# One transfer per head instead of one per pair for spreading the softmax reciprocals, with PE's order searched anew

## The chip, the cores and the metric

The kernel runs on one core of one Trainium2 chip. The metric is the device time of one execution in microseconds. Before the change the median of three runs is 820.94 us (820.1 to 821.65).

## The reference

A block-causal attention (8 batches, 8 heads, 576 positions, head width 64) feeds a mixture of four single-head causal attentions, of which two are chosen per position by a gate. All data are float32.

```python
scores = scale * np.matmul(q, k.transpose(0, 1, 3, 2))
scores = np.where(pos[:, None] // 64 >= pos[None, :] // 64, scores, -1e9)
attn = exp(scores - max);  attn = attn / (sum(attn) + 1e-09)
x = (attn @ v).transpose(0, 2, 1, 3).reshape(B, S, H * D)
...
logits = x @ w_gate                      # the best 2 of 4 experts, softmax over these two
for e in range(4):
    q, k, v = x @ wq[e], x @ wk[e], x @ wv[e]
    a = causal softmax(scale * q @ k.T)
    out += gate[e] * ((a @ v) @ wo[e])
```

## The kernel before

The work comes in 48 pairs: 32 pairs of attention heads (kind "A": 8 batches of 4 pairs) and 16 pairs of experts (kind "M": 8 batches of 2). `add_attention` writes down the tasks of one pair. PE makes the scores of both heads into PSUM (`bank`), DVE masks them and takes the row minimum (`nm`), ACT takes the exponentials into `e` and sums them into `ssum`. The exponentials are transposed for the second product, either by PE (`id,e`) or, for the widest tile, by DVE within blocks (`eI`) and two transfers through DRAM (`dt<-eI`, 640 KB, then four `eTb<-dt` of 160 KB). PE then multiplies with the values into another bank, where positions lie along the free axis and the 64 columns of head 0 and of head 1 lie in partitions 0 to 63 and 64 to 127.

In that layout the division by the softmax sum needs the reciprocal of each position in every one of a head's 64 partitions. The chain for it is: ACT adds epsilon (`f_r1`, `r<-ssum`), DVE takes the reciprocal (`f_r2`) and, for experts, multiplies by the gate (`f_r3`), DVE transposes 32 x 32 blocks (`f_rt`, `rT<-r`), SP writes the result to DRAM (`f_rw`, `dr<-rT`, 16 KB), and SP reads it back spread over the partitions (`f_rd`, `rs<-dr`, 288 KB: 2304 bytes into each of 128 partitions). In DRAM head 0's 576 numbers start at 0 and head 1's at element 640. Then DVE multiplies the product in PSUM by `rs` (`f_p1`, `x<-bank,rs`), which frees the bank; `x` is rounded and its rest kept (`f_p2`, `f_p3`) for the next projections, or (`y`, `yl`) for the output projection with `woh` and `wol`.

There are three `rs` buffers and two of `r`, `rT` and `dr`; the latter come free when the transfer `rs<-dr` that reads `dr` has landed. [...]

Order: `Plan.run` is a list scheduler in Python that runs while the kernel is built. Each task has an engine, a cost, keys (`KEYS`) that set which of the ready tasks goes first, and for transfers a latency `lat` and a ring load. PE's tasks go in the order of the table `LINE`, fixed. The result is one stream per engine, executed in order: an engine that waits holds up all that stands behind it. All input transfers, the turn through `dt` and the reciprocals are issued on SP; the outputs on ACT. Where a helper issues every instruction, all have one line (L327).

## Time and profile before

| what | value |
|---|---|
| median of 3 runs | 820.94 us |
| the profiled execution | 812.63 us |
| its span, first to last instruction | 810.8 us |
| PE, DVE, ACT, POOL busy in it | 616.6, 484.3, 447.4, 185.9 us |
| mean granted TensorE clock | 0.863 |
| mean DMA rate | 150 GB/s (121.84 MB) |

The profile is of one execution. "Busy" counts instructions; a busy PE need not be at its peak, and its matmuls last longer at a lower granted clock. The table of waits says which engine stood still, and what ended its wait; the chain follows the work that ended last back to its start.

### The profile page before, as it was taken

The page shows a single profiled execution, that of the slowest core. Times are in us where ns is not written, and L with a number is a line of the kernel's source. Part 1 is how long each engine was busy: PE and PEld are TensorE (multiplying, and loading weights), DVE is VectorE, ACT ScalarE, POOL GpSimd, SP SyncE. Part 2 cuts the span into 40 slices and gives each one's busy share as a digit, 9 for nine tenths or more (in the row PEclk, how much of TensorE's full clock was granted, in tenths as well). Part 3 has the DMA queues.
Part 4 walks back from the last instruction along what each step waited for, and adds up shares of the span by engine and source line. Part 5 has one row for each costly group of instructions (what it writes and reads, how often), then busy time and mean ns, then how long its engine had stood idle before and what let it go on. Part 6 is the DMA issues. An engine that isn't in the chain of part 4 may idle for free.

```text
span 810.8 us, 19107 instructions
## 1 busy us (share of the span) xinstructions
PE 616.6 (76%) x7235; PEld 560.7 (69%) x7235; DVE 484.3 (60%) x1709; ACT 447.4 (55%) x1502; POOL 185.9 (23%) x272
## 2 busy tenths in 40 slices
PE   7668885589769689669777879696596775968964
PEld 5557784489668588569766778585595665868953
DVE  7466674478547567458665668584484554643931
ACT  6565574368537466457655656564484454543631
POOL 2243040223213123223212222031231132100101
PEclk8869997699978979789889898997798888989997
DMA  6526464546565457455654457384376434532222
GB/s 211 152 86 194 125 207 124 150 132 174 172 202 150 130 145 248 115 171 184 182 188 142 136 166 207 122 236 124 113 223 177 142 89 122 162 83 84 91 75 75
DMA packets 75884, 121.84 MB, mean 150 GB/s; under 512 B 11664, under 2 KB 56208, under 8 KB 75792
## 3 DMA queue, kind: packets, MB, share of 16 engines
q1 hardware_dynamic: 70256, 110.88, 47.1%
q10 hardware_dynamic: 5536, 9.73, 3.5%
q8 instruction: 57, 0.93, 0.5%
q14 instruction: 35, 0.29, 0.1%
HBM read 82.19 MB, written 38.40 MB: 149 GB/s over the span
## 4 chain that ended last, share of the span: by engine, by line
DMA 61%; PE 21%; DVE 9%; SPq 3%; ACT 3%; issue 2%; ACTq 0%; DVEq 0%; POOL 0%
DMA rs<-dr 35%; PE bank L327 21%; DMA dr<-rT 13%; DMA dt<-eI 8%; DMA eTb<-dt 4%; SPq L327 3%; DVE bank L327 3%; DVE x L327 2%; DMA raw<-in_qk_dram 2%; ACT e L327 1%; DVE eI L327 1%; DVE nm L327 0%; DVE r L327 0%; DVE rT L327 0%; ACT el L327 0%
## 5 line engine op out<-in xcount | busy, mean ns | idle before, releaser
L327 ACT ACTIVATE e<-bank,nm 128x448 f32<-128x448 f32 (+3 forms) x384 | 219.0, 579 | 56.8 <-DVE nm L327 54.2
L327 DVE CUSTOM_DVE_ANT_0 bank<-bank,mask_a 128x192 f32<-128x192 f32 (+3 forms) x320 | 154.3, 504 | 19.3 <-PE bank L327 13.8
L327 DVE TENSOR_TENSOR x<-bank,rs 128x256 f32<-128x256 f32 (+1 forms) x144 | 45.7, 349 | 186.4 <-DMA rs<-dr 168.0
L327 PE MATMUL bank<-hl,lo 64*128 64x320 f32 (+2 forms) x352 | 84.9, 437 | 81.8 <-DVE x L327 46.5
L327 PE MATMUL bank<-x,wh 128*128 128x320 f32 (+1 forms) x512 | 111.9, 313 | 0.1
L327 PEld LDWEIGHTS bank<-hl,lo 64*128 64x128 f32 x352 | 46.7, 219 | 88.0 <-issue 38.6
L327 PE MATMUL bank<-id,e 64*128 64x64 f32 x1381 | 71.7, 243 | 32.9 <-ACT e L327 16.2
L327 PEld LDWEIGHTS bank<-id,e 64*128 64x128 f32 x1381 | 63.9, 155 | 44.3 <-ACT e L327 19.8
L327 POOL TENSOR_TENSOR lo<-raw,hl 128x320 fp32r<-128x320 f32 x77 | 65.7, 878 | 124.1 <-ACT hl L327 71.1
L327 PEld LDWEIGHTS bank<-x,wh 128*128 128x128 f32 x512 | 87.1, 200 | 6.3 <-issue 2.5
L327 POOL TENSOR_TENSOR x<-x,x 128x256 fp32r<-128x256 f32 (+1 forms) x55 | 43.6, 798 | 199.3 <-ACT x L327 106.9
L327 PE MATMUL bank<-eTb,va 128*64 128x64 f32 (+2 forms) x1136 | 71.4, 284 | 16.9 <-DMA eTb<-dt 16.0
L327 DVE CUSTOM_DVE_ANT_0 bank<-bank,mask_c 128x448 f32<-128x448 f32 (+4 forms) x160 | 77.6, 501 | 10.7 <-PE bank L327 7.5
L327 PEld LDWEIGHTS bank<-eTb,va 128*64 128x64 f32 x1136 | 67.7, 150 | 21.3 <-ACT x L327 9.4
L327 PE MATMUL bank<-x,wl 128*128 128x320 f32 (+1 forms) x256 | 78.2, 306 | 0.0
L327 ACT ACTIVATION_READ_ACCUMULATOR e<-bank,nm 128x1 f32 x384 | 78.0, 203 | 0.0
L327 PE MATMUL bank<-lo,hl 64*128 64x320 f32 (+2 forms) x352 | 70.4, 354 | 0.0
L327 PE MATMUL bank<-hl 64*128 64x320 f32 (+2 forms) x352 | 70.2, 353 | 0.0
L327 DVE STREAM_TRANSPOSE eI<-e 128x1024 f32<-128x1024 f32 x86 | 61.6, 754 | 11.9 <-DMA dt<-eI 9.3
L327 DVE DVE_READ_ACCUMULATOR2_ANT nm<- 128x1 f32 (+1 forms) x480 | 66.9, 139 | 0.0
L327 PE MATMUL bank<-wh,x 128*128 128x260 f32 x288 | 61.9, 295 | 0.0
L327 PE MATMUL bank<-raw 64*128 64x64 f32 (+4 forms) x320 | 48.9, 398 | 15.4 <-DVE x L327 9.7
(113 smaller groups left out, 1232.6 us busy)
## 6 DMA issues: line engine op xcount, KB each, us to landing
dt<-eI SPq DMA_DIRECT2D x43, 640.0 KB
eTb<-dt SPq DMA_DIRECT2D x172, 160.0 KB
va<-in_v_dram SPq DMA_DIRECT2D x32, 576.0 KB
raw<-in_qk_dram SPq DMA_DIRECT2D x31, 576.0 KB
rs<-dr SPq DMA_DIRECT2D x48, 288.0 KB
out_dram<-ob ACTq DMA_DIRECT2D x32, 256.0 KB
raw<-in_w_dram SPq DMA_DIRECT2D x4, 386.0 KB
out_dram<-ob ACTq DMA_DIRECT2D x8, 128.0 KB
```

Source lines behind the costliest of these rows:

```text
L327: r = f(*args, **kwargs)
```

## The change

`f_rd` issues two transfers, one for each head: 64 partitions from head 0's numbers, then 64 partitions from head 1's. Before, one transfer read both by a pattern whose outermost dimension has size 2. The bytes are the same. The planner's cost of the task on SP goes from 620 to 1150 ns, its latency and load stay. `KEYS` and `LINE` are replaced by tables found for these costs, so tasks move on every engine.

```diff
@@ KEYS, LINE: all numbers new @@
     0, 1, 4, 3, 2, 12, 7, 10, 5, 6, 11, 13, 18, 14, 15, 8, 19, 20, 9, 16, 28, 17, 
-    ... 21, 22, 27, 26, 23, 25, 29, 31, 30, 35, 24, 34, 32, 33, 42, 37, 43, 36,
+    ... 22, 21, 27, 26, 23, 24, 25, 29, 31, 30, 35, 34, 33, 32, 36, 43, 37, 42,
...
         def f_rd(e):
             rs, dr = rs_[rsb.idx], dr_[rb.idx]
-            nc.sync.dma_start(rs, bass.AP(tensor=dr.tensor, offset=dr.offset, ap=[[640, 2], [0, 64], [1, S]]))
+            for h in range(2):
+                nc.sync.dma_start(rs[64 * h:64 * h + 64], bass.AP(tensor=dr.tensor, offset=dr.offset + 640 * h,
+                                                                  ap=[[0, 64], [1, S]]))
...
         t_ = plan.add("S", 570, f_rw, n_, deps=(t_,), lat=1000, load=150)
-        rd = plan.add("S", 620, f_rd, n_, deps=(t_,), get=(rsb,), rel=(rb,), lat=1800, load=900)
+        rd = plan.add("S", 1150, f_rd, n_, deps=(t_,), get=(rsb,), rel=(rb,), lat=1800, load=900)
```

SP, where two pairs issue their `rs` back to back (136 to 147 us in the profile before). Before:

```order
L327 DMA dr_143<-rT_141 4x32x32
L327 DMA dr_142<-rT_140 4x32x32
L327 DMA rs_136<-dr_143 128x1x576
L327 DMA rs_137<-dr_142 128x1x576
L327 DMA va_112<-in_v_dram 128x1152
L327 DMA dt_111<-eI_108 128x4x320
L327 DMA va_113<-in_v_dram 128x1152
```

After:

```order
L327 DMA dr_143<-rT_141 4x32x32
L327 DMA dr_142<-rT_140 4x32x32
L327 DMA rs_136<-dr_143 64x576 x2
L327 DMA rs_137<-dr_142 64x576 x2
L327 DMA dt_111<-eI_108 128x4x320
L327 DMA va_113<-in_v_dram 128x1152
```

Each `rs` is issued in two pieces, and `dt_111` moves ahead of a load of values.

DVE at the same place, where it reads these two `rs` (ISA rows are the masking and the minimum). Before:

```order
L327 TENSOR_TENSOR x_133<-bank_147,rs_135 128x256
L327 ISA bank_149,nm<-bank_149,mask_c 128x448
L327 ISA nm 128x1
L327 TENSOR_TENSOR x_117<-x_133,x_117 128x256
L327 TENSOR_TENSOR x_134<-bank_146,rs_136 128x64
L327 TENSOR_TENSOR x_134<-bank_146,rs_136 128x256
L327 TENSOR_TENSOR x_133<-bank_146,rs_137 128x64
L327 TENSOR_TENSOR x_133<-bank_146,rs_137 128x256
L327 ISA bank_147,nm<-bank_147,mask_c 128x192
```

After:

```order
L327 TENSOR_TENSOR x_133<-bank_148,rs_135 128x256
L327 ISA bank_149,nm<-bank_149,mask_c 128x448
L327 ISA nm 128x1
L327 ISA bank_147,nm<-bank_147,mask_c 128x448
L327 TENSOR_TENSOR x_134<-bank_147,rs_136 128x64
L327 TENSOR_TENSOR x_134<-bank_147,rs_136 128x256
L327 TENSOR_TENSOR x_133<-bank_149,rs_137 128x64
L327 TENSOR_TENSOR x_133<-bank_149,rs_137 128x256
L327 ISA bank_146,nm<-bank_146,mask_c 128x192
```

The multiplications stay side by side, right ahead of the next masking; a subtraction (`x_117`) no longer stands between them and banks change.

PE at that place: the last product before its next scores. Before:

```order
L327 MATMUL bank_147<-eTb_107,va_113 64x128
L327 MATMUL bank_147<-eTb_107,va_113 64x256
L327 MATMUL bank_147<-eTb_107,va_113 64x128 x4
L327 MATMUL bank_147<-eTb_107,va_113 64x64 x3
L327 MATMUL bank_149<-hl_76,lo_78 128x320
L327 MATMUL bank_146<-hl_76,lo_78 128x320
```

After:

```order
L327 MATMUL bank_146<-eTb_107,va_113 64x128
L327 MATMUL bank_146<-eTb_107,va_113 64x256
L327 MATMUL bank_146<-eTb_107,va_113 64x128 x4
L327 MATMUL bank_146<-eTb_107,va_113 64x64 x3
L327 MATMUL bank_148<-hl_76,lo_78 128x320
L327 MATMUL bank_149<-hl_76,lo_78 128x320
```

Here PE's sequence stays and only the banks differ; the scores still write a bank that a multiplication by `rs_137` reads shortly before (146 before, 149 after).

## The prediction

> **What bounds the kernel now.** I read the page's head and its chain first.

> ```profile
> span 810.8 us, 19107 instructions
> PE 616.6 (76%) x7235; PEld 560.7 (69%) x7235; DVE 484.3 (60%) x1709; ACT 447.4 (55%) x1502; POOL 185.9 (23%) x272
> DMA rs<-dr 35%; PE bank L327 21%; DMA dr<-rT 13%; DMA dt<-eI 8%; DMA eTb<-dt 4%; SPq L327 3%; DVE bank L327 3%; DVE x L327 2%; DMA raw<-in_qk_dram 2%; ACT e L327 1%; DVE eI L327 1%; DVE nm L327 0%; DVE r L327 0%; DVE rT L327 0%; ACT el L327 0%
> ```

> No engine is full: PE, the fullest, idles 810.8 − 616.6 = 194 us. The transfer that the change touches is 35% of the chain (284 us), more than PE's work. The table of waits (total us, times, longest) says whom it holds up:

> ```profile
> DVE x L327 <- DMA rs<-dr: 168.0, 33, 10.3
> PE bank L327 <- DVE x L327: 87.1, 22, 9.7
> ACT r L327 <- DMA rs<-dr: 64.2, 13, 9.3
> PE bank L327 <- ACT e L327: 32.5, 13, 8.6
> PE bank L327 <- DMA eTb<-dt: 22.2, 5, 7.0
> PE bank L327 <- ACT eTb L327: 15.6, 6, 5.5
> PE bank L327 <- ACT vm L327: 8.5, 2, 6.8
> PE bank L327 <- POOL ytl L327: 6.2, 1, 6.2
> PE bank L327 <- DVE gsm L327: 4.9, 1, 4.9
> ```

> DVE stands 168 us for `rs`, mean 5.1; PE stands 87 us for the multiplication behind it. ACT stands 64 us because `r` has two buffers, which come free when an older `rs` has landed, and ACT's exponentials stand behind that. One such place in the timeline (start, duration, instruction, idle before it), and the end of the kernel:

> ```profile
> 139.90 1.11 SPq L327 DMA_DIRECT2D rs<-dr  x2
> 149.37 0.56 DVE L327 TENSOR_TENSOR x<-bank,rs 128x64 f32<-128x64 f32 x2 [5.38 <-DMA rs<-dr]
> 155.64 0.56 DVE L327 TENSOR_TENSOR x<-bank,rs 128x64 f32<-128x64 f32 x2 [5.71 <-DMA rs<-dr]
> 156.26 0.64 PE L327 MATMUL bank<-hl,lo 64*128 64x320 f32 x2 [9.68 <-DVE x L327]
> ...
> 778.80 1.18 SPq L327 DMA_DIRECT2D rs<-dr  x2
> 789.51 0.42 DVE L327 TENSOR_TENSOR x<-bank,rs 128x256 f32<-128x256 f32 x1 [10.00 <-DMA rs<-dr]
> 795.50 0.89 DVE L327 TENSOR_TENSOR x<-bank,rs 128x256 f32<-128x256 f32 x3 [5.56 <-DMA rs<-dr]
> ```

> Two `rs` issued half a microsecond apart come 6.27 us apart, and 5.99 us apart at the end, where little else moves. So one `rs` takes 6.0 us of transfer by itself: 288 KB in 6.0 us is 49 GB/s. What a transfer can do here, and what a small one costs, is in the pieces of the chain (start, us from issue to landing) and in the sizes of the page:

> ```profile
> 180.02 4.51 DMA dt<-eI
> 245.19 8.20 DMA rs<-dr
> 777.50 1.96 DMA dr<-rT
> ...
> dt<-eI SPq DMA_DIRECT2D x43, 640.0 KB
> rs<-dr SPq DMA_DIRECT2D x48, 288.0 KB
> dr<-rT SPq DMA_DIRECT2D x48, 16.0 KB
> ```

> 640 KB of `dt<-eI` land 4.51 us after issue, 288 KB of `rs` never sooner than 8.20 in the listed chain, 16 KB in 1.96. `rs` is slow in itself, not for its bytes: it runs on a few of the 16 DMA engines. With 1.96 taken as the fixed part, `dt<-eI` moves 640 KB in 2.55 us, 251 GB/s; at a sixteenth of that per engine (15.7 GB/s), or somewhat more when unhindered, 49 GB/s is two or three engines. The DRAM pattern of `rs` begins with a dimension of size 2, that of `dt` with 128.

> [...]

> **The change part by part.** *Landing of `rs`.* Bounds for the new one from rows: best, 1.96 fixed + 288 KB at 251 GB/s = 1.15 + one more issue; worst, today's 8.2 and more. The issue:

> ```profile
> L327 SPq DMA_DIRECT2D rs<-dr x48: 502/520/3337, 21.3 to 779.5; - x48
> ```

> So 1.96 + 1.15 + 0.52 = 3.6 us. I take 3.6, since the new pattern is like that of `dt` with its partitions outermost. That is 4.6 us less than 8.2, and over 5 less than the usual 9 to 10.

> *DVE and PE.* 33 waits of 5.1 us in the mean, nearly all shorter than 5 to 6, mostly vanish. Of PE's 87.1 us behind them I take nine tenths: 78. Of the waits for `ACT e` (32.5), and for `eTb`, `vm`, `ytl`, `gsm` (15.6 + 8.5 + 6.2 + 4.9 = 35.2) about half stand behind a DVE or ACT that waited for `rs`: 34. Bounds here: none of it, or all 68.

> *The other transfers.* All of SP's traffic shares the 16 engines:

> ```profile
> q1 hardware_dynamic: 70256, 110.88, 47.1%
> 336.32 6.84 SPq L327 DMA_DIRECT2D va<-in_v_dram  x2
> ```

> If `rs` sits on two engines, it holds these for 48 × 6.0 = 288 us, on top of the rest of the traffic, at most 47% of 811 = 381: up to 82% busy where the mean is half. Whatever spreads over all 16 waits for its share on these two, and SP itself is held while issuing (6.84 us for two loads, against 0.35 or so). I take half of PE's 22.2 us for `eTb`: 11. Bounds 0 and 22.

> *Clock.* The table by 20 us windows (PE, PEld, DVE, ACT, POOL busy with counts, granted clock, DMA share, GB/s): the first is a window with stalls, the others are all with PE busy 18 us or more.

> ```profile
> 140.00:160.00 20.00, 10.32 (x134) 9.48 (x133) 8.01 (x29) 6.33 (x20) 4.78 (x7) 0.73 0.42 126
> 100.00:120.00 20.00, 18.41 (x252) 16.80 (x248) 15.26 (x57) 14.05 (x48) 8.11 (x12) 0.88 0.67 207
> 180.00:200.00 20.00, 20.00 (x207) 18.37 (x205) 16.97 (x60) 17.91 (x64) 6.63 (x8) 1.00 0.64 184
> 300.00:320.00 20.00, 20.00 (x292) 18.29 (x290) 17.59 (x65) 16.20 (x55) 7.03 (x11) 1.00 0.80 237
> 420.00:440.00 20.00, 18.44 (x249) 16.15 (x248) 12.71 (x48) 12.47 (x43) 5.34 (x8) 0.95 0.68 192
> 580.00:600.00 20.00, 18.92 (x209) 17.65 (x210) 17.09 (x61) 15.64 (x52) 7.87 (x12) 0.85 0.59 181
> 700.00:720.00 20.00, 18.25 (x217) 16.43 (x217) 12.29 (x45) 10.99 (x39) 0.00 (x0) 1.00 0.59 158
> 760.00:780.00 20.00, 19.11 (x207) 17.02 (x207) 17.34 (x67) 13.27 (x49) 1.71 (x3) 1.00 0.32 105
> ...
> core 0: 810.8 us, clock 0.863
> ```

> Dense windows get 0.95 in the mean, the stalled one 0.73, the whole 0.863. With two thirds of the stalls gone I take 0.92 as the new mean. [...]

> *What is given back.* 48 more issues of 0.52 us are 25 us of SP, which lie beside SP's waits except for the 0.52 counted in each landing; without that cover they are 25 us. The next limits are near: in dense windows DVE and ACT are busy 12 to 18 of 20 us, `dt` and `eTb` are 12% of the chain (97 us), `dr<-rT` still comes ahead of each `rs` with 1.96 us or more. I take a quarter of the 123 us of stalls as coming back under other names: 31. Bounds 0 and about half, 61.

> *The new order* of PE moves few kinds of work at the places shown; I count nothing for it, bounded by the spread of the give-back.

> Sum, on the profiled execution: 812.6 − 78 − 34 − 11 − 19 + 31 = 701.6. The runs' median is 8.3 us above that execution: 710 us.

> **The rivals.** *Another wait takes over.* The turn through `dt` and `eTb`, or DVE's own work, ends the waits instead, and the clock stays. Then only about half of PE's 87 us is won: 812.6 − 44 + 8 = 777. For it speaks that the 43 turns stay as long as `dr` and `dt` queue; against it, that those landings suffer from `rs` as well.

> *PE gets full.* In the seven dense windows 1633 matmuls ran in 140 us; 7235 at that rate take 620 us. With 20 us of start and end and the 8 us: 648. Against it: three engines at 85% or more in order seldom stay so.

> *The halves follow one another, slower.* If the 49 GB/s come from reading the same row of DRAM over and over and not from the number of engines, two transfers gain nothing, and each lands one issue later: 284 us of chain at about 9.7 us a piece are 29 pieces, and 29 × 0.52 = 15 us make 836; if each half in turn takes the full 6 us, 29 × 6 more make 995. It decides if two `rs` still come 6 us apart. Against it: nothing else in the trace is so slow for its bytes, but no other transfer repeats one row, so it can't be excluded. [...]

> **How the numbers follow.** Forecast (670 to 750): 0.62. Another wait (750 to 800): 0.18. PE full (635 to 670): 0.12. Halves follow one another: 0.05. The remaining 0.03 is a gain under 20 us or none, 0.01 of it within 0.2% (what a measurement can tell here) and 0.01 slower by an unlucky order. So faster 0.93, same 0.01, slower 0.06. The range 660 to 785 leaves out the lower part of "PE full", the far end of "another wait" and the slow cases, about 2 in 10; its ends are the sum with all of its terms at their better bounds cut back by half, and 777 with the noise of the runs.

> **What would show it.** Right: `rs` lands 3 to 4.5 us after its second issue, two in a row come 1 to 2 us apart, DVE's wait for `rs` falls under 50 us, PE is busy 82 to 88% of the span at a clock over 0.9, and `dt<-eI` lands in 5 us more often. Wrong on the mechanism: still 6 us between two `rs`. Wrong on the size: `rs` is fast, but PE waits as long for `eTb`, for ACT or for a bank.

## The result, and the profile after

The changed kernel takes 591.1 us (median of four runs, 587.65 to 592.78) against 820.5 us for the kernel before beside it (818.97 to 821.65): a ratio of 0.7199, 95% interval 0.7165 to 0.7234. The forecast was 710 us with a range of 660 to 785, so the gain was right in sign and 119 us too small. Two of the four runs of `e4_k4` below (720.67 and 722.53 us, clock 0.91 where the other two have 0.93) and one of the ten of `e8_more_r` (828.53 us, clock 0.73) are slow runs and stand in no time or ratio here. The profiled execution took 591.24 us. Its head, its row of the DMA queue of SP, its chain and its clock:

```profile
span 589.5 us, 19210 instructions
PE 554.0 (94%) x7235; PEld 506.0 (86%) x7235; DVE 485.1 (82%) x1730; ACT 442.7 (75%) x1494; POOL 177.1 (30%) x259
q1 hardware_dynamic: 71696, 110.89, 65.4%
PE bank L327 60%; DMA rs<-dr 8%; DMA dr<-rT 4%; DMA dt<-eI 4%; SPq L327 3%; DVE bank L327 3%; DMA raw<-in_qk_dram 3%; ACT e L327 2%; DMA eTb<-dt 2%; DVE x L327 1%; DVE eI L327 1%; ACT eTb L327 1%; DMA out_dram<-ob 1%; DVE eTa L327 1%; DVE eTb L327 0%
```

```profile
core 0: 589.5 us, clock 0.985
```

PE is busy 94% of the span where it was 76%, and its work is 60% of the chain where `rs<-dr` was 35%. The span lost 810.8 − 589.5 = 221.3 us in two parts: PE's idle time went from 194.2 to 35.5 us (−158.7), and PE's busy time for the same 7235 matmuls from 616.6 to 554.0 us (−62.6), at a granted clock of 0.985 instead of 0.863. DVE and ACT are busy as long as before (485 and 443 us against 484 and 447).

The table of waits after (total us, times, longest):

```profile
DVE x L327 <- DMA rs<-dr: 23.7, 15, 4.2
ACT r L327 <- DMA rs<-dr: 12.4, 8, 2.7
PE bank L327 <- DVE x L327: 8.4, 10, 2.0
PE bank L327 <- ACT e L327: 7.0, 9, 1.3
PE bank L327 <- DMA eTb<-dt: 1.9, 2, 1.6
PE bank L327 <- ACT eTb L327: 1.8, 3, 0.8
```

DVE's 168.0 us for `rs` are 23.7, and PE's 87.1 us behind them 8.4. PE's waits for `ACT e`, for `ACT eTb` and for the transfer of `eTb` fall to 7.0, 1.8 and 1.9 us. What a reader of the profile before could have seen, but the prediction did not show, is SP's own table of waits. Its two greatest rows, first before and then after:

```profile
SPq L327 <- DMA dt<-eI: 127.2, 26, 11.1
SPq L327 <- DMA dr<-rT: 102.5, 27, 9.4
```

```profile
SPq L327 <- DMA dt<-eI: 65.4, 27, 5.4
SPq L327 <- DMA dr<-rT: 61.3, 32, 4.3
```

SP issues in order. It must see `dt` landed before it issues `eTb<-dt`, and `dr` before `rs<-dr`. Before the change it stood 229.7 us for these two, after it 126.7, though neither transfer was touched.

The place at which two `rs` are issued in a row, and the end of the kernel, as the timeline has them (start, duration, instruction, idle before it):

```profile
106.03 3.68 SPq L327 DMA_DIRECT2D rs<-dr  x4
110.98 0.55 DVE L327 TENSOR_TENSOR x<-bank,rs 128x64 f32<-128x64 f32 x2 [1.79 <-DMA rs<-dr]
112.47 0.56 DVE L327 TENSOR_TENSOR x<-bank,rs 128x64 f32<-128x64 f32 x2 [0.94 <-DMA rs<-dr]
...
569.16 2.41 SPq L327 DMA_DIRECT2D rs<-dr  x4
572.96 0.42 DVE L327 TENSOR_TENSOR x<-bank,rs 128x256 f32<-128x256 f32 x1 [2.86 <-DMA rs<-dr]
574.75 1.10 DVE L327 TENSOR_TENSOR x<-bank,rs 128x256 f32<-128x256 f32 x3 [0.44 <-DMA rs<-dr]
```

The multiplications of the two pairs start 1.5 and 1.8 us apart, where they were 6.3 and 6.0 us apart. And by 20 us windows (span of the window, PE, PEld, DVE, ACT, POOL busy, granted clock, DMA share, GB/s):

```profile
100.00:120.00 20.00, 17.94 (x283) 16.82 (x285) 15.49 (x60) 13.28 (x45) 6.97 (x10) 0.98 0.66 190
140.00:160.00 20.00, 20.00 (x272) 18.43 (x269) 18.36 (x67) 17.11 (x61) 9.17 (x13) 1.00 0.73 218
300.00:320.00 20.00, 18.98 (x257) 16.90 (x257) 17.60 (x65) 16.04 (x51) 6.96 (x10) 1.00 0.85 248
```

Windows as dense as the best of before are now the rule: PE is busy 18 us or more in 24 of the 29 whole windows, 23 of them at clock 1.00, where it was in 7 of the first 40 before.

### The profile page after: what moved, and what is told of

Same layout as the page of the kernel before. It is cut to its first block, busy times and chain, and to the rows that moved or that the text cites. A ratio compares the mean times of both kernels' runs of the same rounds, so it can differ in the third digit from the quotient of the medians.

```text
span 589.5 us, 19210 instructions
## 1 busy us (share of the span) xinstructions
PE 554.0 (94%) x7235; PEld 506.0 (86%) x7235; DVE 485.1 (82%) x1730; ACT 442.7 (75%) x1494; POOL 177.1 (30%) x259
## 2 busy tenths in 40 slices
DMA packets 77324, 121.84 MB, mean 207 GB/s; under 512 B 13104, under 2 KB 57648, under 8 KB 77232
## 4 chain that ended last, share of the span: by engine, by line
PE 60%; DMA 21%; DVE 8%; ACT 5%; SPq 3%; issue 2%; ACTq 0%; POOL 0%; DVEq 0%
PE bank L327 60%; DMA rs<-dr 8%; DMA dr<-rT 4%; DMA dt<-eI 4%; SPq L327 3%; DVE bank L327 3%; DMA raw<-in_qk_dram 3%; ACT e L327 2%; DMA eTb<-dt 2%; DVE x L327 1%; DVE eI L327 1%; ACT eTb L327 1%; DMA out_dram<-ob 1%; DVE eTa L327 1%; DVE eTb L327 0%
## 5 line engine op out<-in xcount | busy, mean ns | idle before, releaser
L327 ACT ACTIVATE e<-bank,nm 128x192 f32<-128x192 f32 (+3 forms) x384 | 219.5, 581 | 23.0 <-DVE nm L327 20.6
L327 DVE CUSTOM_DVE_ANT_0 bank<-bank,mask_a 128x192 f32<-128x192 f32 (+3 forms) x320 | 154.4, 501 | 15.3 <-PE bank L327 8.9
L327 PE MATMUL bank<-x,wh 128*128 128x320 f32 (+1 forms) x512 | 105.6, 300 | 0.8 <-ACT e L327 0.7
L327 POOL TENSOR_TENSOR lo<-raw,hl 128x320 fp32r<-128x320 f32 x77 | 65.7, 879 | 89.8 <-issue 28.3
L327 PEld LDWEIGHTS bank<-x,wh 128*128 128x128 f32 x512 | 81.5, 188 | 5.4 <-issue 1.0
L327 DVE CUSTOM_DVE_ANT_0 bank<-bank,mask_c 128x320 f32<-128x320 f32 (+4 forms) x160 | 77.5, 501 | 5.7 <-PE bank L327 2.7
L327 PE MATMUL bank<-hl,lo 64*128 64x320 f32 (+2 forms) x352 | 75.8, 388 | 5.7 <-POOL lo L327 2.8
L327 ACT ACTIVATION_READ_ACCUMULATOR e<-bank,nm 128x1 f32 x384 | 78.3, 204 | 0.0
L327 PE MATMUL bank<-x,wl 128*128 128x320 f32 (+1 forms) x256 | 75.4, 295 | 0.0
L327 PEld LDWEIGHTS bank<-id,e 64*128 64x128 f32 x1381 | 58.5, 144 | 18.6 <-ACT e L327 7.8
L327 PE MATMUL bank<-id,e 64*128 64x64 f32 x1381 | 66.3, 230 | 7.8 <-ACT e L327 4.9
L327 DVE TENSOR_TENSOR x<-bank,rs 128x256 f32<-128x256 f32 (+1 forms) x144 | 45.4, 347 | 28.6 <-DMA rs<-dr 23.7
L327 PE MATMUL bank<-eTb,va 128*64 128x64 f32 (+2 forms) x1136 | 64.6, 265 | 3.2 <-DMA eTb<-dt 1.9
L327 PEld LDWEIGHTS bank<-eTb,va 128*64 128x64 f32 x1136 | 61.0, 137 | 7.0 <-issue 4.4
L327 POOL TENSOR_TENSOR x<-x,x 128x256 fp32r<-128x256 f32 (+1 forms) x49 | 38.9, 800 | 92.7 <-ACT x L327 60.7
L327 DVE DVE_READ_ACCUMULATOR2_ANT nm<- 128x1 f32 (+1 forms) x480 | 66.6, 139 | 0.0
L327 PE MATMUL bank<-hl 64*128 64x320 f32 (+2 forms) x352 | 63.1, 315 | 0.0
L327 PE MATMUL bank<-lo,hl 64*128 64x320 f32 (+2 forms) x352 | 63.1, 315 | 0.0
L327 DVE STREAM_TRANSPOSE eI<-e 128x1024 f32<-128x1024 f32 x86 | 61.5, 754 | 1.5 <-DMA dt<-eI 0.7
L327 PE MATMUL bank<-wh,x 128*128 128x260 f32 x288 | 58.4, 286 | 0.0
L327 POOL TENSOR_TENSOR lo<-mops,hl 128x288 fp32r<-128x288 f32 (+1 forms) x47 | 33.0, 726 | 63.2 <-ACT hl L327 34.5
L327 ACT COPY eTb<-bank 128x192 f32<-128x192 f32 (+2 forms) x185 | 43.1, 319 | 10.2 <-PE bank L327 9.7
```

The lines of the kernel that those rows point to most:

```text
L327: r = f(*args, **kwargs)
```

## The experiments

Each ratio is to runs of the kernel before on the same chip. Two causes were to be told apart throughout. Theory A: `rs` on two engines harms by what else has to share these engines. Theory B: it harms by its own lateness.

**The split or the order?** `e1_split_old_order` is the kernel before with its old tables and only this edit:

```diff
-            nc.sync.dma_start(rs, bass.AP(tensor=dr.tensor, offset=dr.offset, ap=[[640, 2], [0, 64], [1, S]]))
+            for h in range(2):
+                nc.sync.dma_start(rs[64 * h:64 * h + 64], bass.AP(tensor=dr.tensor, offset=dr.offset + 640 * h,
+                                                                  ap=[[0, 64], [1, S]]))
```

> The kernel before with only the two transfers a head put in; every engine keeps the order of before. Theory 1, the number of DMA engines that rs runs on decides (two before, sixteen after): 590 to 625 us, nearly all of the 230 us gain, rs landing in 3 to 5 us. Theory 2, the new order of tasks brought much of it: 680 to 760 us.

`e2_joint_new_order` is the changed kernel with that edit turned back, so with the new order on every engine.

> The changed kernel with only the one joint transfer put back; every engine keeps the new order. Theory 1: 790 to 850 us, as before or worse, since the new order counts on an rs that lands early. Theory 2: 650 to 750 us.

The first took 598.35 us, ratio 0.73 (0.726 to 0.7339); the second 818.81, ratio 1.0021 (0.9988 to 1.0054). PE's row of the second, and its DVE wait for `rs`:

```profile
PE 624.4 (77%) x7235; PEld 565.9 (70%) x7235; DVE 489.5 (60%) x1730; ACT 445.5 (55%) x1494; POOL 177.7 (22%) x259
```

```profile
DVE x L327 <- DMA rs<-dr: 152.5, 30, 9.3
```

It looks as the kernel before. The split makes the gain; the new order saves about 7 us more (598.35 against 591.1) with the split and nothing without it.

**Two pieces, or more engines?** `e3_cols` cuts the transfer in two by columns and leaves the outermost size at 2:

```diff
-            for h in range(2):
-                nc.sync.dma_start(rs[64 * h:64 * h + 64], bass.AP(tensor=dr.tensor, offset=dr.offset + 640 * h,
-                                                                  ap=[[0, 64], [1, S]]))
+            for c in (0, 288):
+                nc.sync.dma_start(rs[:, c:c + 288], bass.AP(tensor=dr.tensor, offset=dr.offset + c, ap=[[640, 2], [0, 64], [1, 288]]))
```

> The changed kernel, new order, with two transfers a pair as in the change, but cut by columns: each brings 288 of the 576 numbers of both heads, so its DRAM pattern still begins with a dimension of size 2. Issues and bytes are those of the change. Theory 1 (engines): 790 to 850 us, two rs still about 6 us apart. Theory 3, that two smaller transfers are faster by being smaller: 590 to 650 us.

It took 849.32 us, ratio 1.0369 (1.0324 to 1.0413): slower than one transfer. So two issues and two pieces by themselves don't make the gain. Its rows are also half as long (1152 bytes); no run shows whether that has a part in the loss. The end of its timeline:

```profile
764.80 6.45 SPq L327 DMA_DIRECT2D rs<-dr  x4
780.32 0.42 DVE L327 TENSOR_TENSOR x<-bank,rs 128x256 f32<-128x256 f32 x1 [10.70 <-DMA rs<-dr]
```

`e4_k4` and `e4_k8` keep two transfers of 64 partitions and change only how the pattern that repeats a row is written: with 4 or 8 outermost instead of 64.

```diff
-                                                                  ap=[[0, 64], [1, S]]))
+                                                                  ap=[[0, 4], [0, 16], [1, S]]))
```

> The changed kernel, new order, one transfer a head, the repetition of 64 written as 4 by 16, so that the DRAM pattern begins with 4. Theory 1 in its form that the outermost size sets the engines: rs on four engines, 3 us of transfer for a pair, landing at 5 to 6 us, 610 to 680 us. Theory 4, that joining both heads in one pattern was what made rs slow, whatever its outermost size: as the change, 585 to 597 us.

> As the run with 4 by 16, but the repetition written as 8 by 8. If rs runs on as many engines as the outermost size (two gave 819 us, four 716), eight bring 1.5 us of transfer for a pair and 620 to 670 us. If four was slow for another reason than its engines (a third dimension in the pattern), eight is as slow: 700 to 730 us.

They took 709.5 us (the middle of 708.45 and 710.62), ratio 0.8655 (0.8628 to 0.8682), and 618.88 us, ratio 0.7547 (0.7509 to 0.7585). Four engines are slower than the 610 to 680 us expected, eight a little faster than 620 to 670. What tells the number of engines here is the packets of SP's queue, of `e4_k4` and then of `e4_k8`:

```profile
q1 hardware_dynamic: 70544, 110.88, 58.3%
```

```profile
q1 hardware_dynamic: 70928, 110.88, 63.4%
```

The kernel before has 70256 packets, with the same bytes. The excess is 288, 672 and, for the change, 1440, which is 48 times 6, 14 and 30. A pair's transfers thus have 6, 14 and 30 packets more than the old one. In the lists of packets of the traces before and after, SP's queue has 4848 and 6288 packets of 4 bytes, which is the whole excess, while a row of `rs` is one packet of 2304 (6144 of these in both). The pages count 11664 packets under 512 bytes before and 11953, 12336 and 13104 in the three: 289 (one of them of another queue), 672 and 1440 more. That fits two transfers on 4, 8 and 16 engines against one on 2, if each engine adds one small packet (2 × 4 − 2, 2 × 8 − 2, 2 × 16 − 2); this reading is meant wherever engines are counted here. `e3_cols` fits too: its queue has 76496 packets, 48 × 130 more than before, which is 128 rows and 2 small packets for the second piece (the page has 96 more under 512 bytes, 48 × 2), so each piece ran on two engines. With the same bytes the times by engines are 819 (two), 710 (four), 619 (eight) and 591 us (sixteen).

**The load on two engines without a late `rs`.** `e6_load2` adds to the changed kernel, behind each pair's `rs`, a copy of 288 KB that nobody waits for, written with 2 outermost; `e7_load16` is its control, with the partitions outermost.

```diff
+            sp = spare_[len(extra) % 4]
+            extra.append(real.sync.dma_start(bass.AP(tensor=sp.tensor, offset=sp.offset, ap=[[64 * S, 2], [S, 64], [1, S]]), wh[:, 0, 0:S].bitcast(F32)))
```

> The changed kernel with a dummy transfer behind each pair's rs that nobody waits for: 288 KB from the projection weights in SBUF to a spare place in DRAM, in a pattern that begins with 2 and so loads two engines for about 6 us; rs itself keeps its sixteen. Theory A, the two loaded engines made every other transfer late, and that was a large part of the loss: 680 to 780 us. Theory B, it was the landing of rs itself, in line with DVE's multiplication: 595 to 640 us, though a later rs can queue behind an earlier dummy.

> The control to the dummy on two engines: the same 288 KB, issued at the same places, with the partitions outermost and so over sixteen engines. Both theories: 592 to 615 us, the price of the extra bytes (13.8 MB on 122) and of 48 more issues on SP.

They took 622.78 (0.7594, 0.7549 to 0.764) and 617.88 us (0.7526, 0.7483 to 0.7569). The first pair doesn't test the theory: both have 78608 packets in SP's queue, so the pattern of `e6_load2`, whose two halves lie one behind the other in memory, ran on sixteen engines as well. What `e7_load16` does give is the price of the bytes and issues of 48 copies: about 27 us, a little over the expectation. `e6b_load2` leaves a gap between the halves (`65 * S` in place of `64 * S`) and adds the copy only behind every second pair.

> The dummy transfer again, now really on two engines (its DRAM rows leave a gap between the halves, so that the pattern begins with 2) and only behind every second pair, 24 in all; rs keeps its sixteen engines. 24 times 6 us on two engines bring these from some 400 to some 545 us of work. Theory A, load on two engines makes all other transfers late and that was a large part of the loss: 650 to 760 us. Theory B, the landing of rs itself decides: 595 to 630 us.

It took 693.23 us, ratio 0.8476 (0.8416 to 0.8536). Theory A said so, B did not. Its row of SP's queue, its head, its SP waits and the waits for `rs` and `eTb`:

```profile
q1 hardware_dynamic: 74816, 117.97, 58.4%
PE 586.0 (85%) x7235; PEld 536.3 (78%) x7235; DVE 487.2 (71%) x1730; ACT 443.6 (64%) x1494; POOL 176.7 (26%) x259
```

```profile
SPq L327 <- DMA dt<-eI: 110.1, 24, 9.7
SPq L327 <- DMA dr<-rT: 105.2, 34, 7.7
```

```profile
DVE x L327 <- DMA rs<-dr: 36.4, 13, 7.1
PE bank L327 <- DMA eTb<-dt: 29.6, 7, 6.3
```

The queue has 3120 packets more than in the change, 24 × 130 (128 rows and 2 small packets; 48 more under 512 bytes), so this copy did run on two engines. In `e6_load2` and `e7_load16` it has 48 × 144 more (128 rows and 16; 768 more under 512 bytes). Twenty-four copies cost 102 us. Half the price of `e7_load16`, an estimated 13 us of it, is what their bytes and issues cost on sixteen engines, so about 89 us are due to the two engines. SP stands for `dt` and `dr` 215.3 us, 88.6 more than in the changed kernel and nearly as much as before the change, and a further 16.2 us for the copies themselves, while DVE waits for `rs` only 13 us more. So the load reaches PE mostly by the other transfers: PE waits 29.6 us for `eTb`, where it waited 1.9. How much of this is the late `dt` itself, and how much SP's standing for it, isn't separated here.

**A late `rs` without the load.** `e9_hop` lets each pair's `dr` be copied once more within DRAM (16 KB) and reads `rs` from the copy, on sixteen engines (SP's queue has 73232 packets, 48 × 32 more than in the change, 768 of them under 512 bytes: 16 more for each hop, and none for `rs`).

```diff
+            hp = hop_[rb.idx]
+            nc.sync.dma_start(hp, dr)
             for h in range(2):
-                nc.sync.dma_start(rs[64 * h:64 * h + 64], bass.AP(tensor=dr.tensor, offset=dr.offset + 640 * h,
+                nc.sync.dma_start(rs[64 * h:64 * h + 64], bass.AP(tensor=hp.tensor, offset=hp.offset + 640 * h,
```

> The changed kernel with one more small transfer (16 KB, DRAM to DRAM, sixteen engines) between the write of the reciprocals and the two rs, so that each rs lands some 2 to 2.5 us later and no engine has noticeably more to do. Theory B, the landing decides: by the row of engine counts (2.3 us later with four engines cost 125 us) 660 to 720 us. Theory A, load on few engines: 595 to 625 us.

It took 695.55 us, ratio 0.8501 (0.8454 to 0.8548), as B said. But SP stands during the hop:

```profile
SPq L327 <- DMA hop<-dr: 106.8, 48, 6.2
DVE x L327 <- DMA rs<-hop: 76.5, 23, 6.7
```

and all of its other transfers stand behind it. `e11_block` separates this: `rs` is read from `dr` first, and only then SP issues the hop and a tiny transfer that waits for it.

```diff
                                                                   ap=[[0, 64], [1, S]]))
+            hp, hq = hop_[rb.idx], hoq_[rb.idx]
+            real.sync.dma_start(hp, dr)
+            real.sync.dma_start(hq[0:16, 0:16], hp[0:16, 0:16])
```

> The changed kernel, where behind each pair's two transfers for rs SP issues a copy of 16 KB within DRAM and then a tiny transfer that waits for that copy. So SP stands still for about 2.2 us a pair as in e9_hop, but rs is no later than in the changed kernel. If the lateness of rs was what cost e9_hop its 104 us: 595 to 640 us. If SP's standing still was: 670 to 700 us. Between them both have a part.

It took 699.33 us, ratio 0.8566 (0.8508 to 0.8623), as much as `e9_hop`:

```profile
SPq L1051 <- DMA hop<-dr: 111.4, 48, 4.1
SPq L327 <- DMA dr<-rT: 88.2, 32, 5.3
```

```profile
DVE x L327 <- DMA rs<-dr: 48.1, 17, 5.7
```

So what cost 104 us in `e9_hop` comes also when `rs` doesn't wait for the hop. This is not wholly clean. The second of two `rs` in a row is issued behind the first one's hop and is late too (DVE waits 48.1 us for `rs` where it waited 23.7). And SP issues two transfers more a pair, besides its 2.3 us of standing (111.4 us for 48). The 108 us are the price of all of this together; the share of SP's standing alone is not shown.

**Lateness with nothing held.** `e12_touch` makes `rs` usable later by a task of POOL, which copies the landed `rs` onto itself in twelve small pieces; `e13_aside` makes the same copies into a tile that nobody reads.

```diff
+            for i in range(12): real.gpsimd.tensor_copy(rs[:, i::12], rs[:, i::12])
```

> The changed kernel, where POOL copies each landed rs onto itself in twelve small pieces before DVE may multiply with it: rs is usable some 2 to 2.5 us later (estimate from POOL's 0.2 us for a 128x64 copy), and neither SP nor a DMA engine does more. To be read against e13_aside. If the lateness of rs by itself costs time: 48 times about 2.2 us, so 70 to 120 us over e13_aside. If only a blocked SP queue and slowed neighbours cost: at most 20 us over e13_aside.

> Control for e12_touch: the same twelve small copies on POOL behind each rs, but into a tile that nobody reads, so that DVE's multiplication doesn't wait for them. What POOL's added work costs by making its other outputs late: 595 to 640 us by both theories.

They took 714.05 (0.8703, 0.8636 to 0.8771) and 725.74 us (0.886, 0.8812 to 0.8908). The control failed: it is slower than the kernel that it controls. In both, POOL, which is also in order, stood for `rs` with work behind it that PE needed, and the control's copies, all into one small tile, keep POOL busy longer (156.3 us against 124.0). Here are the waits of `e13_aside`:

```profile
POOL aside L1048 <- DMA rs<-dr: 246.5, 37, 17.3
PE bank L327 <- POOL lo L327: 85.6, 14, 14.9
```

`e14_touch_late` and `e15_aside_late` have eight copies, at the place where DVE's first multiplication with this `rs` stands (`f_p1`).

> As e12_touch, but with eight small copies of rs onto itself (8 x 0.27 = 2.2 us), put into POOL's stream where DVE's first multiplication with this rs stands, so that POOL stands little for rs. To be read against e15_aside_late. If the lateness of rs by itself costs time: 60 to 110 us over e15_aside_late. If not: at most 20 us over it.

> Control for e14_touch_late: the same eight copies at the same places, into a tile that nobody reads, so that DVE waits for none of them: 595 to 650 us by both theories.

They took 627.58 (0.7652, 0.76 to 0.7703) and 611.44 us (0.7449, 0.7417 to 0.7482). The waits of the first, with its copies (count, busy us, mean ns):

```profile
L1155 POOL COPY rs<-rs 128x48 f32<-128x48 f32 x384 | 82.2, 271 | 98.3 <-DMA rs<-dr 98.1
```

```profile
DVE x L327 <- POOL rs L1155: 69.8, 36, 7.1
PE bank L327 <- DVE x L327: 26.3, 18, 3.1
```

and those of the control:

```profile
L1156 POOL COPY aside<-rs 128x48 f32<-128x48 f32 x384 | 106.0, 276 | 103.0 <-DMA rs<-dr 81.4
DVE x L327 <- DMA rs<-dr: 16.2, 11, 4.0
PE bank L327 <- DVE x L327: 9.3, 8, 2.6
```

The eight copies overlap (384 of 271 ns would be 104 us one behind the other) and take 1.7 us a pair together (82.2 us for 48), not the 8 × 0.27 = 2.2 us expected. DVE waits 54 us more than in the control (69.8 − 16.2), which is as much as `e9_hop` added to the change (76.5 − 23.7 = 53). PE waits behind it 17 us more (26.3 − 9.3), and the kernel is 16 us longer than the control. But the control is not the same work: its copies all go into one tile and take 2.2 us a pair (106.0 us for 48), so it holds POOL longer and is itself 20 us over the change. The price of the lateness is thus bounded from two sides: at least the 16 us over the control, and at most the 36 us over the change (627.58 − 591.1). That is a sixth to a third of the 104 us which about as long a wait of DVE came with when SP was held too.

`e16_touch_more` and `e17_aside_more` do the same with sixteen copies, which take 3.4 us a pair in the first (162.8 us busy) and 4.4 in the control (209.9).

> As e14_touch_late with sixteen copies instead of eight: rs is usable about 16 x 0.27 = 4.3 us later, the size of what the joint transfer loses. To be read against e17_aside_more. If lateness by itself is cheap and SP's queue is what counts: 30 to 45 us over e17_aside_more (twice the 16 us of e14_touch_late, or a little more). If its price grows fast once the slack is used up: 80 to 150 us over it.

> Control for e16_touch_more: the same sixteen copies at the same places into a tile that nobody reads. By both theories 620 to 680 us, from 611 for eight copies and more time in which POOL is late with its other outputs.

They took 695.71 (0.8493, 0.843 to 0.8556) and 680.57 us (0.8321, 0.8266 to 0.8376): 15 us apart, less than either theory said. The control is 89 us over the change on its own, and what waits already for POOL can't be delayed much by `rs`, so this pair bounds the price of 3.4 us only loosely: at least 15 us, and at most the 105 us that lie between 695.71 and the change.

**More buffers.** `e8_more_r` gives the kernel before a third buffer of `r`, `rT` and `dr` (with 48 instead of 60 of `nm`, for room), `e10_after_r3` gives it to the changed kernel.

```diff
-                 x=6, y=3, yt=2, x32=2, rs=3, r=2, gate=2, lg=1, ob=2, nm=60, el=2)
+                 x=6, y=3, yt=2, x32=2, rs=3, r=3, gate=2, lg=1, ob=2, nm=48, el=2)
```

> The kernel before with three buffers r, rT and dr in place of two (and 48 of 60 columns for the row minima), rs still one transfer; its planner then orders tasks a little otherwise. ACT stood 64 us before it could write r. If the missing buffer, not the landing of rs, cost the time: 740 to 780 us. If the landing decides: 805 to 830 us, and the wait moves to DVE.

> The changed kernel with three buffers r, rT and dr in place of two (48 of 60 columns for the row minima). ACT still waits 12.4 us for r in the changed kernel. If these waits are in line: 578 to 588 us. If PE, busy 94%, bounds: 588 to 596 us, no difference. The planner orders ACT and DVE anew around it, so up to 600 us is possible.

They took 818.33 us, ratio 0.9987 (0.9948 to 1.0026), and 604.79, ratio 0.7398 (0.7366 to 0.743). Two waits of `e8_more_r`:

```profile
ACT r L327 <- DMA rs<-dr: 4.8, 1, 4.8
DVE x L327 <- DMA rs<-dr: 180.9, 36, 9.8
```

ACT's 64.2 us for a free `r` are gone, DVE's wait grew by 13 us, and the time stayed. The buffers were no limit of their own. In the changed kernel the other order that comes with them is 14 us slower, and no version tried beats the change.

## Why the prediction was wrong, step by step

*What came out as forecast.* The mechanism: `rs` ran on two engines and runs on sixteen, by the packets of 4 bytes (4848 before, 6288 after), and the time falls with the engines: 819, 710, 619 and 591 us for two, four, eight and sixteen. The signs listed: two `rs` come 1.5 and 1.8 us apart (forecast 1 to 2), DVE's wait for `rs` is 23.7 us (under 50), the clock 0.985 (over 0.9). `rs` lands in under 4 us in five of the ten pieces of the chain, as in the first two here (start, us from issue to landing), while the others take up to 7. The last sign, `dt<-eI` landing in 5 us more often, isn't seen in the chain, where its three pieces take 6.8 to 8.7:

```profile
96.20 3.03 DMA rs<-dr
109.11 3.24 DMA rs<-dr
...
322.03 7.02 DMA rs<-dr
```

The first term, −78 us for PE behind DVE's `x`, measured −78.7, in part by luck: DVE's waits were said to be nearly all shorter than 5 to 6 us, but ten of the 33 were longer than 6, up to 10.3. The 251 GB/s for `dt<-eI` takes a KB as 1000 bytes and the 49 GB/s for `rs` as 1024; taken alike it is 257, and the 1.15 us stay. The rival "halves follow one another" fell at once: it decided by 6 us between two `rs`, and they come 1.5 and 1.8 us apart.

*What failed.* PE busy is 94%, above the forecast's 82 to 88%, and 591.1 us lie below every range that the prediction listed. Four of the five terms were mis-sized, all in one direction:

| term | forecast | measured | read from |
|---|---|---|---|
| PE behind DVE's `x` | −78 | −78.7 | 87.1 to 8.4 |
| PE for `ACT e`, `eTb`, `vm`, `ytl`, `gsm` | −34 | −58.9 | 67.7 to 8.8 |
| PE for the transfer `eTb<-dt` ("the other transfers") | −11 | −20.3 | 22.2 to 1.9 |
| the clock | −19 | −62.6 | PE busy 616.6 to 554.0 |
| what is given back, under all names | +31 | −0.8 | what is left of 221.3 |

The worst is *what is given back*. The prediction took a quarter of the vanished stalls as coming back and got none: PE idles 35.5 us in all, and every wait of PE that the prediction listed went down. Of the next limits that it named, DVE and ACT at 82% and 75% did not stop PE. The others, `dt`, `eTb` and `dr`, it counted as if they were independent of `rs`. They were its victims: SP stood 103 us longer for `dt` and `dr` before the change (229.7 against 126.7), the kernel with an untouched `rs` and a load on two engines stands nearly as long and loses 102 us (`e6b_load2`), and holding SP behind `rs` costs about as much (`e11_block`, with its further issues and a somewhat later second `rs`). The prediction named this, "whatever spreads over all 16 waits for its share on these two", and `e6b_load2` shows its effect (PE waits 29.6 us for `eTb` where it waited 1.9, and 8.6 in `e7_load16`, whose copies are on sixteen), but it was priced by PE's one visible row for `eTb`, at 11 us. PE's other waits were booked as halves on the same ground; nearly all of them went.

The second is *the clock*. Had PE's 616.6 us shrunk wholly by the ratio of the clocks, 616.6 × 0.863/0.985 = 540 would be left; 554 were measured. The prediction had 0.92 instead of 0.985 and then halved the effect: its 19 us are half of 616.6 × (1 − 0.863/0.92) = 38. No run shows a ground for this halving; what the runs showed in its place is that, with stalls nearly gone, the clock went to 0.985 and four fifths of full scaling came (62.6 of 76). The stalls of PE and its slower matmuls go together in all kernels here: the clock records of the traces before and after know only full and half speed, and by the mean clock the time at half speed is an estimated 222 us before ((1 − 0.863)/0.5 × 810.8), 102 with four engines (0.928, 708.8 us), 36 with eight (0.971, 613.1 us) and 18 after, and the time at full speed lies between 572 and 607 us in these four. Since no run kept the clock up through the stalls, this shows how they go together and not how much each would be alone.

*The rival that came true* is "PE gets full", at 0.12. Its kind was right and its price of 648 us was not: it took the rate of matmuls from windows of which two had a clock of 0.85 and 0.88, and added 20 us for start and end. The argument against it, that three engines at 85% or more in order seldom stay so, is borne out by the windows before (in none of the first 40 were PE, DVE and ACT all busy 17 of 20 us; nearest are 20.00, 16.97 and 17.91), but did not hold after the change: five of 29 are above 17 in all three, and PE reached 94% with DVE at 82% and ACT at 75%.

*What stays open.* Of the 228 us between two and sixteen engines, about 89 can be had from two engines' load alone, by 24 copies, half as many as there are `rs`. Lateness alone of 1.7 us a pair costs 16 to 36 us, of 3.4 us between 15 and 105. Two engines make `rs` later by an estimated 4 to 6 us (most pieces of the chain take 8 to 11 us to landing before, and 3 to 7 after), and no run has that lateness by itself. How the whole is shared between load and lateness isn't settled. That SP's queue carries most of the load's effect is argued from `e6b_load2` and `e11_block` and not shown; a kernel that issues `dt` and `dr` from another engine's queue wasn't tried.

## What to carry to other kernels

When one transfer is slow for its bytes, look first at the outermost size of its DRAM pattern, with which its engines and its price went here (2, 4, 8 and 64 outermost gave 819, 710, 619 and 591 us; where the two halves of `e6_load2` joined in memory, 2 cost no more than its control: 622.78 against 617.88), and count the engine time that it takes from every other transfer as well as its own landing. Read the waits of the issuing queue: SP, which issues in order and waits for landings, stood 229.7 us for `dt` and `dr` here with the slow transfer and 126.7 without it, and PE waited under many names that looked independent (87.1 us for `x`, 32.5 for `ACT e`, 22.2 for `eTb`; then 8.4, 7.0 and 1.9). Where those waits have one common cause, take them off together, and the granted clock with them (0.863 to 0.985 here), instead of discounting each.
